# All matmuls of a fused convolution and feed-forward kernel in 64-row tiles

## Chip, cores, metric

The kernel runs on one core of one Trainium2 chip. The metric is device time in microseconds (us). The kernel before takes 831.15 us (median of 4 fast runs, 828.9 to 833.99). A ratio is the mean time of one kernel's fast runs over the mean time of the other's fast runs of the same rounds, so it is not quite the ratio of the medians quoted beside it.

Words used below. A *stage* is 512 tokens of each half of the batch, 1024 in all; there are 32, and a 33rd turn of the loop that only finishes the last output. A *unit* is a sixteenth of a stage on TensorE: one chunk of 128 hidden features of this stage, and half a block of 128 tokens of the previous stage's output. *Row tiling* is how many of the 128 rows of TensorE's array a matmul takes: all 128, or 64, and then two matmuls (a *pair*) can sit side by side. A *bank* is a part of PSUM, the memory that matmuls write to. The *span* runs from a core's first instruction to its last. PE is TensorE, PEld its weight loads, DVE VectorE, ACT ScalarE, POOL GpSimd, SP SyncE.

## The reference, cut

```python
# x: (8, 4096, 192), weight: (8 heads, 7 taps); 24 channels to a head
w = softmax(weight)                            # over the 7 taps of each head
conv[b,s,d] = sum_k w[head(d),k] * x[b, s-6+k, d]   # zeros ahead of the first token
h = conv @ w_in                                # 192 -> 2048
g = h * sigmoid(beta * h)
out = g @ w_out                                # 2048 -> 192
```

The contraction of the first product is 192 long: one and a half times the 128 rows of the array.

## The kernel before

The two halves of the batch (`h`) are computed together. The input tile of a stage has three column groups: group 0 and 1 are channels 0 to 127 of half 0 and of half 1 (128 partitions each), group 2 is channels 128 to 191 of both halves, half 0 on partitions 0 to 63 and half 1 on 64 to 127. So the hidden product is two matmuls of 128 rows and a pair of 64 rows that sit beside each other in the array.

```python
def hidden(s, fc):                 # one chunk of 128 hidden features
    ph = psum_h.tile([128, 2, TOK], FP32)             # bufs=3, one bank per half
    w = w_in_s[:, :, fc * 128 : (fc + 1) * 128]
    for h in range(2):
        nc.tensor.matmul(ph[:, h, :], w[:, 0, :], ct[:, h, :], start=True, stop=False)
    for h in range(2):
        rows = slice(h * DB, (h + 1) * DB)            # DB = 64
        nc.tensor.matmul(ph[:, h, :], w[rows, 1, :], ct[rows, 2, :], start=False, stop=True)
    nc.scalar.activation(g[:, fc, :, :], ph, AF.Silu, scale=beta[:, fc : fc + 1])

def output(s, part):               # half a block of 128 tokens: 8 of 16 chunks
    # ... (cut: which block, which half; po takes two blocks, one bank, bufs=2)
    for fc in range(half * NF // 2, (half + 1) * NF // 2):
        nc.tensor.matmul(po[:, q % 2, :], g[:, fc, h, q * BLK : (q + 1) * BLK],
                         w_out_s[:, fc, :], start=(fc == 0), stop=(fc == NF - 1))
    if part % 4 == 3:
        nc.vector.tensor_copy(osb[:, q - 1 : q + 1, :], po)
    # ... (cut: store after every fourth block)

for s in range(N_ST + 1):
    ops = conv_ops(s + 1)          # 14: seven taps on groups 0-1 (1024 wide), seven on group 2 (512)
    for u in range(NF):            # 16 units
        # ... (cut: weight preparation in stage 0)
        hidden(s, u)
        output(s - 1, u)
        if u < len(ops):
            ops[u]()               # VectorE: a tap of the next stage's convolution
        # ... (cut: cast of stage s+3 to bf16 in DRAM, transposing load of stage s+2)
```

The seven taps are one multiplication (TENSOR_SCALAR), five multiply-adds (SCALAR_TENSOR_TENSOR) and one addition (TENSOR_TENSOR) on VectorE.

Of the kernel before, what the change touches and what calls it, by code (L numbers as in the profile page):

```python
# [8 lines left out]
FP32 = mybir.dt.float32  # L9
BF16 = mybir.dt.bfloat16  # L10
AF = mybir.ActivationFunctionType
ALU = mybir.AluOpType
# [3 lines left out]
def kernel(  # L16
# [15 lines left out]
    nc = tc.nc  # L32

    B, S, D = x.shape
    H, K = weight.shape
    F = moe_w_in.shape[1]
    group = D // H
    DA = 128
    DB = D - DA
    TOK = 512  # L40
    NF = F // 128
    PAD = K - 1
    HALO = 16
    CHUNKS = S // TOK
    N_ST = (B // 2) * CHUNKS
    BLK = 128
    N_BLK = TOK // BLK


    x_v = x.rearrange("(h p) s d -> p s h d", h=2)  # L50
# [4 lines left out]
    consts = ctx.enter_context(tc.tile_pool(name="consts", bufs=1))  # L55
    setup = ctx.enter_context(tc.tile_pool(name="setup", bufs=1))
    xd_pool = ctx.enter_context(
        tc.tile_pool(name="xd", bufs=4, space=bass.MemoryType.DRAM)
    )
    xt_pool = ctx.enter_context(tc.tile_pool(name="xt", bufs=3))  # L60
    ct_pool = ctx.enter_context(tc.tile_pool(name="ct", bufs=2))
    g_pool = ctx.enter_context(tc.tile_pool(name="g", bufs=2))
    osb_pool = ctx.enter_context(tc.tile_pool(name="osb", bufs=3))
    psum_h = ctx.enter_context(
        tc.tile_pool(name="psum_h", bufs=3, space=bass.MemoryType.PSUM)
    )
    psum_o = ctx.enter_context(
        tc.tile_pool(name="psum_o", bufs=2, space=bass.MemoryType.PSUM)
    )
# [6 lines left out]
    def cast(s):  # L76
        p, c = divmod(s, CHUNKS)
        r0 = HALO if c == 0 else 0
        t0 = c * TOK - HALO + r0
        t1 = (c + 1) * TOK  # L80
        xd = xd_pool.tile([HALO + TOK, 3, DA], BF16, name="xd")
        nc.gpsimd.dma_start(out=xd[r0:, 0:2, :], in_=x_v[p, t0:t1, :, 0:DA])  # L82
        nc.gpsimd.dma_start(  # L83
            out=xd[r0:, 2, :].rearrange("t (h d) -> t h d", h=2),
            in_=x_v[p, t0:t1, :, DA:D],
        )
        xds[s] = xd

    def xpose(s):
        r0 = HALO if s % CHUNKS == 0 else 0  # L90
        xd = xds.pop(s)
        xt = xt_pool.tile([128, 3, HALO + TOK], BF16, name="xt")
        if r0:
            nc.vector.memset(xt[:, :, 0:HALO], 0.0)
        nc.sync.dma_start_transpose(  # L95
            xt[:, :, r0:], xd[r0:, :, :].rearrange("t c d -> t (c d)")
        )
        xts[s] = xt


    cw = consts.tile([128, 2, K], FP32)
    full = DA // group
    rest = DA - full * group

    def heads(rows, h0, h1, n):
        nc.scalar.dma_start(
            out=rows,
            in_=weight[h0:h1, :].unsqueeze(1).to_broadcast((h1 - h0, n, K)),
        )

    cast(0)
    heads(cw[0 : full * group, 0, :], 0, full, group)
    heads(cw[full * group : DA, 0, :], full, full + 1, rest)
    for h in range(2):
        o = h * DB
        heads(cw[o : o + group - rest, 1, :], full, full + 1, group - rest)
        heads(cw[o + group - rest : o + DB, 1, :], full + 1, H, group)
    beta_q = setup.tile([NF, 128], FP32)
    nc.scalar.dma_start(out=beta_q, in_=moe_beta.rearrange("(c p) -> c p", p=128))
    xpose(0)  # L120
# [5 lines left out]
    FW = F // NW  # L126
    w_in_raw = []
    for i in range(NW):
        raw = setup.tile([128, 2, FW], FP32, name=f"w_in_raw{i}")
        cols = slice(i * FW, (i + 1) * FW)  # L130
        nc.sync.dma_start(out=raw[:, 0, :], in_=moe_w_in[0:DA, cols])  # L131
        nc.sync.dma_start(out=raw[0:DB, 1, :], in_=moe_w_in[DA:D, cols])
        nc.sync.dma_start(out=raw[DB:128, 1, :], in_=moe_w_in[DA:D, cols])  # L133
        w_in_raw.append(raw)
    w_out_raw = setup.tile([128, NF, D], FP32)
    nc.sync.dma_start(  # L136
        out=w_out_raw, in_=moe_w_out.rearrange("(c p) d -> p c d", p=128)
# [2 lines left out]
    cast(2)  # L140
    xpose(1)

    nmax = setup.tile([128, 2], FP32)
    nc.vector.reduce_max(nmax, cw, axis=mybir.AxisListType.X, negate=True)  # L144
    for j in range(2):
        nc.scalar.activation(cw[:, j, :], cw[:, j, :], AF.Exp, bias=nmax[:, j : j + 1])  # L146
    ssum = setup.tile([128, 2], FP32)
    nc.vector.reduce_sum(ssum, cw, axis=mybir.AxisListType.X)
    rsum = setup.tile([128, 2], FP32)
    nc.vector.reciprocal(rsum, ssum)  # L150
    w_last = consts.tile([128, 2], FP32)
    nc.vector.tensor_tensor(w_last, cw[:, :, K - 1], rsum, ALU.mult)
    r_last = setup.tile([128, 2], FP32)
    nc.vector.reciprocal(r_last, cw[:, :, K - 1])
    for j in range(2):
        nc.vector.tensor_scalar_mul(cw[:, j, :], cw[:, j, :], r_last[:, j : j + 1])

    pb = psum_o.tile([128, NF], FP32, name="po")
    nc.tensor.transpose(pb, beta_q, ident)  # L159
    beta = consts.tile([128, NF], FP32)  # L160
    nc.vector.tensor_copy(beta, pb)  # L161
    beta_r = setup.tile([128, NF], FP32)
    nc.vector.reciprocal(beta_r, beta)

    w_in_s = consts.tile([128, 2, F], BF16)

    def prep_w_in(i):
        cols = slice(i * FW, (i + 1) * FW)
        for j in range(2):
            nc.vector.tensor_scalar_mul(  # L170
                w_in_s[:, j, cols], w_in_raw[i][:, j, :], w_last[:, j : j + 1]
            )

    w_out_s = consts.tile([128, NF, D], BF16)
# [8 lines left out]

    def conv_ops(s):
        xt = xts.pop(s)
        ct = ct_pool.tile([128, 3, TOK], BF16, name="ct")
        cts[s] = ct
        ops = []
        for j, cs in ((0, slice(0, 2)), (1, slice(2, 3))):

            def tap(k, j=j, cs=cs):
                src = xt[:, cs, HALO - PAD + k : HALO - PAD + k + TOK]
                dst = ct[:, cs, :]
                if k == 0:
                    nc.vector.tensor_scalar_mul(dst, src, cw[:, j, 0:1])  # L195
                elif k < K - 1:
                    nc.vector.scalar_tensor_tensor(  # L197
                        out=dst,
                        in0=src,
                        scalar=cw[:, j, k : k + 1],  # L200
                        in1=dst,
                        op0=ALU.mult,
                        op1=ALU.add,
                    )
                else:
                    nc.vector.tensor_tensor(dst, src, dst, ALU.add)  # L206

            ops += [lambda k=k, tap=tap: tap(k) for k in range(K)]
        return ops

    gs = {}

    def hidden(s, fc):
        ct, g = cts[s], gs[s]
        ph = psum_h.tile([128, 2, TOK], FP32, name="ph")
        w = w_in_s[:, :, fc * 128 : (fc + 1) * 128]
        for h in range(2):
            nc.tensor.matmul(ph[:, h, :], w[:, 0, :], ct[:, h, :], start=True, stop=False)  # L218
        for h in range(2):
            rows = slice(h * DB, (h + 1) * DB)  # L220
            nc.tensor.matmul(  # L221
                ph[:, h, :], w[rows, 1, :], ct[rows, 2, :], start=False, stop=True
            )
        nc.scalar.activation(g[:, fc, :, :], ph, AF.Silu, scale=beta[:, fc : fc + 1])  # L224

    pos, osbs = {}, {}

    def output(s, part):

        blk, half = divmod(part, 2)  # L230
        h, q = divmod(blk, N_BLK)
        g = gs[s]
        if part % 4 == 0:
            pos[s] = psum_o.tile([128, 2, D], FP32, name="po")
        if part % 8 == 0:
            osbs[s] = osb_pool.tile([128, N_BLK, D], FP32, name="osb")
        po, osb = pos[s], osbs[s]
        for fc in range(half * NF // 2, (half + 1) * NF // 2):
            nc.tensor.matmul(  # L239
                po[:, q % 2, :],  # L240
                g[:, fc, h, q * BLK : (q + 1) * BLK],
                w_out_s[:, fc, :],
                start=(fc == 0),
                stop=(fc == NF - 1),
            )
        if part % 4 == 3:
            nc.vector.tensor_copy(osb[:, q - 1 : q + 1, :], po)  # L247
        if part % 8 == 7:
            p, c = divmod(s, CHUNKS)
            nc.sync.dma_start(out=out_v[h, p, c], in_=osb)  # L250
# [4 lines left out]
    for s in range(N_ST + 1):  # L255
        if s < N_ST:
            gs[s] = g_pool.tile([128, NF, 2, TOK], BF16, name="g")
        ops = conv_ops(s + 1) if s + 1 < N_ST else []
        for u in range(NF):
            if s == 0 and u % (NF // NW) == 0:  # L260
                prep_w_in(u // (NF // NW))
            if s < N_ST:
                hidden(s, u)
            if s > 0:
                output(s - 1, u)
            if u < len(ops):
                ops[u]()
            if s == 0:
                prep_w_out(u)
            if u == 0 and s + 3 < N_ST:  # L270
                cast(s + 3)
            if u == 1 and s + 2 < N_ST:
                xpose(s + 2)
# [30 lines left out]
```

## Time and profile before

| what | before |
|---|---|
| median of 4 runs | 831.15 us |
| span of the profiled run | 829.9 us |
| first output matmul starts | 61.67 us |
| unit (period of the hidden matmuls) | 1.520 us, in all of the stream |
| last matmul starts | 825.21 us |

The unit is the time from one chunk's first hidden matmul to the next chunk's, taken from the start times in the trace; from the first output matmul on there are 495, and all lie within 0.01 us of 1.520.

These are lines of the page of the kernel before: busy time by engine (share of the span, instructions), the shares of the chain of waits by engine and line, and groups of instructions (busy us, mean ns of one, idle before).

```profile
PE 784.3 (95%) x6145; PEld 445.7 (54%) x6145; DVE 462.8 (56%) x613; ACT 572.7 (69%) x516; POOL 82.5 (10%) x70
...
PE 93%; DMA 4%; DVE 2%; SPq 1%; issue 0%; POOL 0%; POOLq 0%
PE po L239 47%; PE ph L218 26%; PE ph L221 20%; DMA xt<-xd 2%; DMA w_in_raw_107<-in_moe_w_in_dram 1%; DVE ct L197 1%; DMA xd<-in_x_dram 1%; DVE w_out_s L177 1%; DVE w_in_s L170 0%; SPq L95 0%; SPq L133 0%; SPq L131 0%; DVE ct L195 0%; DVE ct L206 0%; SPq L136 0%
...
L224 ACT ACTIVATE g<-ph,beta 128x1024 bf16<-128x1024 f32 x512 | 569.6, 1114 | 233.6 <-PE ph L221 233.6
L239 PE MATMUL po<-w_out_s,g 128*128 128x192 bf16 x4096 | 424.0, 247 | 0.0
...
L218 PE MATMUL ph<-ct,w_in_s 128*128 128x512 bf16 x1024 | 308.2, 383 | 31.1 <-DVE w_in_s L170 31.1
...
L247 DVE COPY osb<-po 128x384 f32<-128x384 f32 x128 | 71.4, 557 | 329.0 <-PE po L239 329.0
L221 PE MATMUL ph<-ct,w_in_s 64*128 64x512 bf16 x1024 | 201.7, 391 | 0.8 <-DVE w_in_s L170 0.8
```

PE is busy 95% of the span and 93% of the chain of waits; ACT has a 1.11 us activation to do in each unit. L218 are the 128-row hidden matmuls, L221 the 64-row ones, L239 the output. The mean ns of a matmul is its time from start to modelled end, with overlap, so it is not what a matmul costs in a stream. For that, starts are compared. This is the timeline of one unit (start us, us, engine, line, operation; `x2` merges two of a kind):

```profile
399.78 0.59 PE L218 MATMUL ph<-ct,w_in_s 128*128 128x512 bf16 x2
400.30 0.10 PEld L221 LDWEIGHTS <-w_in_s 64*128 64x128 bf16 x2 [0.42 <-issue]
400.30 0.39 PE L221 MATMUL ph<-ct,w_in_s 64*128 64x512 bf16 x2
400.62 0.61 PEld L239 LDWEIGHTS <-g 128*128 128x128 bf16 x8 [0.23 <-issue]
400.63 0.83 PE L239 MATMUL po<-w_out_s,g 128*128 128x192 bf16 x8
...
401.30 0.59 PE L218 MATMUL ph<-ct,w_in_s 128*128 128x512 bf16 x2
401.50 0.56 DVE L247 COPY osb<-po 128x384 f32<-128x384 f32 x1 [3.62 <-PE po L239]
```

From the first L218 at 399.78 to L221 at 400.30 pass 0.52 us for two matmuls of 512 columns. From L221 at 400.30 to L239 at 400.63 pass 0.33 us for a pair that runs as one. From L239 at 400.63 to the next L218 at 401.30 pass 0.67 us for eight matmuls of 192 columns. The single starts in the trace say what the stream costs: two 128-row matmuls start 216 ns apart (399.776 and 399.992), the two of the 64-row pair 3 ns apart (400.304 and 400.307), and the output matmuls 82.5 ns apart (the first two 93). Three times 216 and eight times 82.5 ns is 1.308 us. The unit takes 1.520. The missing 0.212 us lies at the two changes between 128-row and 64-row matmuls, ahead of the pair and behind it: PEld L221 and PEld L239 stand idle ahead of their loads (0.42 and 0.23 us, given to "issue", no semaphore), where the other loads run ahead of the matmul that they serve.

### The profile page before, as it was taken

The page shows a single profiled execution, that of the slowest core. Times are in us where ns is not written, and L with a number is a line of the kernel's source. Part 1 is how long each engine was busy: PE and PEld are TensorE (multiplying, and loading weights), DVE is VectorE, ACT ScalarE, POOL GpSimd, SP SyncE. Part 2 cuts the span into 40 slices and gives each one's busy share as a digit, 9 for nine tenths or more (in the row PEclk, how much of TensorE's full clock was granted, in tenths as well). Part 3 has the DMA queues.
Part 4 walks back from the last instruction along what each step waited for, and adds up shares of the span by engine and source line. Part 5 has one row for each costly group of instructions (what it writes and reads, how often), then busy time and mean ns, then how long its engine had stood idle before and what let it go on. Part 6 is the DMA issues. An engine that isn't in the chain of part 4 may idle for free.

```text
span 829.9 us, 13854 instructions
## 1 busy us (share of the span) xinstructions
PE 784.3 (95%) x6145; PEld 445.7 (54%) x6145; DVE 462.8 (56%) x613; ACT 572.7 (69%) x516; POOL 82.5 (10%) x70
## 2 busy tenths in 40 slices
PE   0279999999999999999999999999999999999997
PEld 0015555555555555555555555555555555555556
DVE  2696665555656556565555656555565665555601
ACT  1267777777777777777777777777777777777772
POOL 8389800000000000000000000000000000000000
PEclk9989999999999999999999999999999999999999
DMA  9999991210322221122222112222201322220111
GB/s 143 222 169 179 182 120 41 58 53 25 59 58 46 53 58 43 35 59 58 39 58 59 36 42 59 58 39 58 59 28 51 59 59 39 58 54 25 39 39 59
DMA packets 157341, 55.60 MB, mean 67 GB/s; under 512 B 121425, under 2 KB 156257, under 8 KB 157281
## 3 DMA queue, kind: packets, MB, share of 16 engines
q1 hardware_dynamic: 88592, 41.77, 22.1%
q0 software_dynamic: 68352, 12.93, 18.9%
q8 instruction: 48, 0.79, 0.4%
q10 hardware_dynamic: 337, 0.02, 0.0%
q14 instruction: 12, 0.10, 0.0%
HBM read 29.54 MB, written 38.09 MB: 81 GB/s over the span
## 4 chain that ended last, share of the span: by engine, by line
PE 93%; DMA 4%; DVE 2%; SPq 1%; issue 0%; POOL 0%; POOLq 0%
PE po L239 47%; PE ph L218 26%; PE ph L221 20%; DMA xt<-xd 2%; DMA w_in_raw_107<-in_moe_w_in_dram 1%; DVE ct L197 1%; DMA xd<-in_x_dram 1%; DVE w_out_s L177 1%; DVE w_in_s L170 0%; SPq L95 0%; SPq L133 0%; SPq L131 0%; DVE ct L195 0%; DVE ct L206 0%; SPq L136 0%
## 5 line engine op out<-in xcount | busy, mean ns | idle before, releaser
L224 ACT ACTIVATE g<-ph,beta 128x1024 bf16<-128x1024 f32 x512 | 569.6, 1114 | 233.6 <-PE ph L221 233.6
L239 PE MATMUL po<-w_out_s,g 128*128 128x192 bf16 x4096 | 424.0, 247 | 0.0
L239 PEld LDWEIGHTS <-g 128*128 128x128 bf16 x4096 | 312.4, 98 | 112.2 <-issue 112.2
L218 PE MATMUL ph<-ct,w_in_s 128*128 128x512 bf16 x1024 | 308.2, 383 | 31.1 <-DVE w_in_s L170 31.1
L197 DVE SCALAR_TENSOR_TENSOR ct<-xt,cw,ct 128x1024 bf16<-128x1024 bf16 (+1 forms) x320 | 325.1, 1016 | 8.8
L247 DVE COPY osb<-po 128x384 f32<-128x384 f32 x128 | 71.4, 557 | 329.0 <-PE po L239 329.0
L221 PE MATMUL ph<-ct,w_in_s 64*128 64x512 bf16 x1024 | 201.7, 391 | 0.8 <-DVE w_in_s L170 0.8
L221 PEld LDWEIGHTS <-w_in_s 64*128 64x128 bf16 x1024 | 49.3, 93 | 221.3 <-issue 217.8
L218 PEld LDWEIGHTS <-w_in_s 128*128 128x128 bf16 x1024 | 91.3, 98 | 36.8 <-DVE w_in_s L170 32.3
L82 POOL DMA_DIRECT2D xd<-in_x_dram x32 | 42.6, 1330 | 12.4 <-DMA xd<-in_x_dram 11.6
L83 POOL DMA_DIRECT2D xd<-in_x_dram x32 | 42.5, 1327 | 8.3 <-DMA xd<-in_x_dram 7.9
L206 DVE TENSOR_TENSOR ct<-xt,ct 128x1024 bf16<-128x1024 bf16 x64 | 35.7, 557 | 2.1
L195 DVE TENSOR_SCALAR ct<-xt,cw 128x1024 bf16<-128x1024 bf16 x64 | 27.6, 431 | 14.1 <-DMA xt<-xd 13.3
L177 DVE TENSOR_SCALAR w_out_s<-w_out_raw,beta_r 128x192 bf16<-128x192 f32 x16 | 8.9, 568 | 0.0
L159 PE MATMUL po<-ident,beta_q 16*128 16x16 f32 x1 | 0.3, 254 | 9.2 <-DMA beta_q<-in_moe_beta_dram 9.2
L146 ACT ACT_TABLE_LOAD x1 | 1.3, 1283 | 6.1 <-DMA cw<-in_weight_dram 6.1
L159 PEld LDWEIGHTS po<-ident,beta_q 16*128 16x128 f32 x1 | 0.2, 176 | 9.1 <-issue 9.1
L144 DVE TENSOR_REDUCE nmax<-cw 128x2 f32<-128x14 f32 x1 | 0.2, 168 | 7.7 <-DMA cw<-in_weight_dram 7.7
L224 ACT ACT_TABLE_LOAD x1 | 1.3, 1283 | 1.5 <-DVE beta L161 1.5
L170 DVE TENSOR_SCALAR w_in_s<-w_in_raw_115,w_last 128x512 bf16<-128x512 f32 x2 | 1.5, 800 | 0.0
L146 ACT ACTIVATE cw<-cw,nmax 128x7 f32<-128x7 f32 x2 | 0.5, 294 | 1.4 <-DVE nmax L144 1.4
L170 DVE TENSOR_SCALAR w_in_s<-w_in_raw_111,w_last 128x512 bf16<-128x512 f32 x2 | 1.5, 774 | 0.0
(16 smaller groups left out, 4.7 us busy)
## 6 DMA issues: line engine op xcount, KB each, us to landing
out_dram<-osb SPq DMA_DIRECT2D x64, 384.0 KB, 3.0
xd<-in_x_dram POOLq DMA_DIRECT2D x28, 264.0 KB, 10.1
xd<-in_x_dram POOLq DMA_DIRECT2D x28, 132.0 KB, 10.2
w_out_raw<-in_moe_w_out_dram SPq DMA_DIRECT2D x1, 1536.0 KB, 12.8
xd<-in_x_dram POOLq DMA_DIRECT2D x4, 256.0 KB, 9.1
xd<-in_x_dram POOLq DMA_DIRECT2D x4, 128.0 KB, 8.7
xt<-xd SPq DMA_TRANSPOSE x32, 4.6
w_in_raw_103<-in_moe_w_in_dram SPq DMA_DIRECT2D x1, 256.0 KB
```

The costliest lines, as they stand in the source:

```text
L82: nc.gpsimd.dma_start(out=xd[r0:, 0:2, :], in_=x_v[p, t0:t1, :, 0:DA])
L83: nc.gpsimd.dma_start(out=xd[r0:, 2, :].rearrange("t (h d) -> t h d", h=2), in_=x_v[p, t0:t1, :, DA:D],)
L170: nc.vector.tensor_scalar_mul(w_in_s[:, j, cols], w_in_raw[i][:, j, :], w_last[:, j : j + 1])
L177: nc.vector.tensor_scalar_mul(w_out_s[:, c, :], w_out_raw[:, c, :], beta_r[:, c : c + 1])
L195: nc.vector.tensor_scalar_mul(dst, src, cw[:, j, 0:1])
L197: nc.vector.scalar_tensor_tensor(out=dst, in0=src, scalar=cw[:, j, k : k + 1], in1=dst, op0=ALU.mult, op1=ALU.add,)
L206: nc.vector.tensor_tensor(dst, src, dst, ALU.add)
L218: nc.tensor.matmul(ph[:, h, :], w[:, 0, :], ct[:, h, :], start=True, stop=False)
L221: nc.tensor.matmul(ph[:, h, :], w[rows, 1, :], ct[rows, 2, :], start=False, stop=True)
L224: nc.scalar.activation(g[:, fc, :, :], ph, AF.Silu, scale=beta[:, fc : fc + 1])
L239: nc.tensor.matmul(po[:, q % 2, :], g[:, fc, h, q * BLK : (q + 1) * BLK], w_out_s[:, fc, :], start=(fc == 0), stop=(fc == NF - 1),)
L247: nc.vector.tensor_copy(osb[:, q - 1 : q + 1, :], po)
```

## The change

The intent: no change of the array's row tiling is left in the loop. Each partition half holds one batch half in all three groups of 64 channels, so the hidden product is three 64-row pairs. The contraction of the output product (128 hidden features) is split as well: rows 0 to 63 into one PSUM bank, rows 64 to 127 into another, and VectorE adds the two. So the two tiles of a pair never write to one bank. `po` grows to two banks, so `ph` goes from three buffers to two. Every group of 64 channels now has its own heads on the same partitions, so the taps are 21 of width 512 instead of 14, and they are spread over all 16 units.

```diff
 def hidden(s, fc):
-    w = w_in_s[:, :, fc * 128 : (fc + 1) * 128]
-    for h in range(2):
-        nc.tensor.matmul(ph[:, h, :], w[:, 0, :], ct[:, h, :], start=True, stop=False)
-    for h in range(2):
-        rows = slice(h * DB, (h + 1) * DB)
-        nc.tensor.matmul(
-            ph[:, h, :], w[rows, 1, :], ct[rows, 2, :], start=False, stop=True
-        )
+    cols = slice(fc * 128, (fc + 1) * 128)
+    for j in range(NG):                       # NG = 3 groups of DG = 64 channels
+        for h in range(2):
+            rows = slice(h * DG, (h + 1) * DG)
+            nc.tensor.matmul(ph[:, h, :], w_in_s[rows, j, cols], ct[rows, j, :],
+                             start=(j == 0), stop=(j == NG - 1))
...
 def output(s, part):
+    b = quarter // 2
+    for fc in range((quarter % 2) * NF // 2, (quarter % 2 + 1) * NF // 2):
+        for r in range(2):
+            rows = slice(r * 64, (r + 1) * 64)
+            nc.tensor.matmul(po[:, r, b * D : (b + 1) * D],
+                             g[rows, fc, h, (q + b) * BLK : (q + b + 1) * BLK],
+                             w_out_s[rows, fc, :],
+                             start=(fc == 0), stop=(fc == NF - 1))
+    if quarter == 3:
+        dst = osb[:, q : q + 2, :].rearrange("p b d -> p (b d)")
+        nc.vector.tensor_copy(dst, po[:, 0, 0 : 2 * D])
+        nc.vector.tensor_tensor(dst, po[:, 1, 0 : 2 * D], dst, ALU.add)
...
             hidden(s, u)
             output(s - 1, u)
-            if u < len(ops):
-                ops[u]()
+            for op in ops[u * len(ops) // NF : (u + 1) * len(ops) // NF]:
+                op()
... (cut: psum_h bufs 3 -> 2; po two banks; the casts write the new layout in pieces of
...  64 channels; w_in is loaded to both partition halves, 3 MB instead of 2 MB; the
...  conv weights are loaded in 14 small loads instead of 6; scaling per group)
```

More of the change, by code (lines that the diff above doesn't have):

```diff
@@ L37 @@
     group = D // H
-    DA = 128
-    DB = D - DA
+    DG = 64
+    NG = D // DG
     TOK = 512
@@ L64 @@
     psum_h = ctx.enter_context(
-        tc.tile_pool(name="psum_h", bufs=3, space=bass.MemoryType.PSUM)
+        tc.tile_pool(name="psum_h", bufs=2, space=bass.MemoryType.PSUM)
     )
@@ L80, in cast @@
         t1 = (c + 1) * TOK
-        xd = xd_pool.tile([HALO + TOK, 3, DA], BF16, name="xd")
-        nc.gpsimd.dma_start(out=xd[r0:, 0:2, :], in_=x_v[p, t0:t1, :, 0:DA])
-        nc.gpsimd.dma_start(
-            out=xd[r0:, 2, :].rearrange("t (h d) -> t h d", h=2),
-            in_=x_v[p, t0:t1, :, DA:D],
-        )
+        xd = xd_pool.tile([HALO + TOK, NG, 2, DG], BF16, name="xd")
+        for h in range(2):
+            nc.gpsimd.dma_start(
+                out=xd[r0:, :, h, :],
+                in_=x_v[p, t0:t1, h, :].rearrange("t (c d) -> t c d", c=NG),
+            )
         xds[s] = xd
@@ L91, in xpose @@
         xd = xds.pop(s)
-        xt = xt_pool.tile([128, 3, HALO + TOK], BF16, name="xt")
+        xt = xt_pool.tile([128, NG, HALO + TOK], BF16, name="xt")
         if r0:
@@ L95, in xpose @@
         nc.sync.dma_start_transpose(
-            xt[:, :, r0:], xd[r0:, :, :].rearrange("t c d -> t (c d)")
+            xt[:, :, r0:], xd[r0:].rearrange("t c h d -> t (c h d)")
         )
         xts[s] = xt
-    cw = consts.tile([128, 2, K], FP32)
-    full = DA // group
-    rest = DA - full * group
-    def heads(rows, h0, h1, n):
-        nc.scalar.dma_start(
-            out=rows,
-            in_=weight[h0:h1, :].unsqueeze(1).to_broadcast((h1 - h0, n, K)),
-        )
+    cw = consts.tile([128, NG, K], FP32)
     cast(0)
-    heads(cw[0 : full * group, 0, :], 0, full, group)
-    heads(cw[full * group : DA, 0, :], full, full + 1, rest)
     for h in range(2):
-        o = h * DB
-        heads(cw[o : o + group - rest, 1, :], full, full + 1, group - rest)
-        heads(cw[o + group - rest : o + DB, 1, :], full + 1, H, group)
+        for c in range(NG):
+            d = c * DG
+            while d < (c + 1) * DG:
+                head = d // group
+                end = min((head + 1) * group, (c + 1) * DG)
+                n = 1
+                if d % group == 0 and end - d == group:
+                    n = ((c + 1) * DG - d) // group
+                    end = d + n * group
+                o = h * DG - c * DG
+                nc.scalar.dma_start(
+                    out=cw[o + d : o + end, c, :],
+                    in_=weight[head : head + n, :]
+                    .unsqueeze(1)
+                    .to_broadcast((n, (end - d) // n, K)),
+                )
+                d = end
     beta_q = setup.tile([NF, 128], FP32)
@@ L128 @@
     for i in range(NW):
-        raw = setup.tile([128, 2, FW], FP32, name=f"w_in_raw{i}")
+        raw = setup.tile([128, NG, FW], FP32, name=f"w_in_raw{i}")
         cols = slice(i * FW, (i + 1) * FW)
-        nc.sync.dma_start(out=raw[:, 0, :], in_=moe_w_in[0:DA, cols])
-        nc.sync.dma_start(out=raw[0:DB, 1, :], in_=moe_w_in[DA:D, cols])
-        nc.sync.dma_start(out=raw[DB:128, 1, :], in_=moe_w_in[DA:D, cols])
+        for h in range(2):
+            nc.sync.dma_start(
+                out=raw[h * DG : (h + 1) * DG, :, :],
+                in_=moe_w_in[:, cols].rearrange("(c d) f -> d c f", c=NG),
+            )
         w_in_raw.append(raw)
@@ L141 @@
     xpose(1)
-    nmax = setup.tile([128, 2], FP32)
+    nmax = setup.tile([128, NG], FP32)
     nc.vector.reduce_max(nmax, cw, axis=mybir.AxisListType.X, negate=True)
-    for j in range(2):
+    for j in range(NG):
         nc.scalar.activation(cw[:, j, :], cw[:, j, :], AF.Exp, bias=nmax[:, j : j + 1])
-    ssum = setup.tile([128, 2], FP32)
+    ssum = setup.tile([128, NG], FP32)
     nc.vector.reduce_sum(ssum, cw, axis=mybir.AxisListType.X)
-    rsum = setup.tile([128, 2], FP32)
+    rsum = setup.tile([128, NG], FP32)
     nc.vector.reciprocal(rsum, ssum)
-    w_last = consts.tile([128, 2], FP32)
+    w_last = consts.tile([128, NG], FP32)
     nc.vector.tensor_tensor(w_last, cw[:, :, K - 1], rsum, ALU.mult)
-    r_last = setup.tile([128, 2], FP32)
+    r_last = setup.tile([128, NG], FP32)
     nc.vector.reciprocal(r_last, cw[:, :, K - 1])
-    for j in range(2):
+    for j in range(NG):
         nc.vector.tensor_scalar_mul(cw[:, j, :], cw[:, j, :], r_last[:, j : j + 1])
-    pb = psum_o.tile([128, NF], FP32, name="po")
+    pb = psum_o.tile([128, 2, TOK], FP32, name="po")[:, 0, 0:NF]
     nc.tensor.transpose(pb, beta_q, ident)
@@ L163 @@
     nc.vector.reciprocal(beta_r, beta)
-    w_in_s = consts.tile([128, 2, F], BF16)
+    w_in_s = consts.tile([128, NG, F], BF16)
     def prep_w_in(i):
         cols = slice(i * FW, (i + 1) * FW)
-        for j in range(2):
+        for j in range(NG):
             nc.vector.tensor_scalar_mul(
@@ L185, in conv_ops, with tap @@
         xt = xts.pop(s)
-        ct = ct_pool.tile([128, 3, TOK], BF16, name="ct")
+        ct = ct_pool.tile([128, NG, TOK], BF16, name="ct")
         cts[s] = ct
         ops = []
-        for j, cs in ((0, slice(0, 2)), (1, slice(2, 3))):
-            def tap(k, j=j, cs=cs):
-                src = xt[:, cs, HALO - PAD + k : HALO - PAD + k + TOK]
-                dst = ct[:, cs, :]
+        for j in range(NG):
+            def tap(k, j=j):
+                src = xt[:, j, HALO - PAD + k : HALO - PAD + k + TOK]
+                dst = ct[:, j, :]
                 if k == 0:
@@ L215, in hidden @@
         ph = psum_h.tile([128, 2, TOK], FP32, name="ph")
-        w = w_in_s[:, :, fc * 128 : (fc + 1) * 128]
-        for h in range(2):
-            nc.tensor.matmul(ph[:, h, :], w[:, 0, :], ct[:, h, :], start=True, stop=False)
-        for h in range(2):
-            rows = slice(h * DB, (h + 1) * DB)
-            nc.tensor.matmul(
-                ph[:, h, :], w[rows, 1, :], ct[rows, 2, :], start=False, stop=True
-            )
+        cols = slice(fc * 128, (fc + 1) * 128)
+        for j in range(NG):
+            for h in range(2):
+                rows = slice(h * DG, (h + 1) * DG)
+                nc.tensor.matmul(
+                    ph[:, h, :],
+                    w_in_s[rows, j, cols],
+                    ct[rows, j, :],
+                    start=(j == 0),
+                    stop=(j == NG - 1),
+                )
         nc.scalar.activation(g[:, fc, :, :], ph, AF.Silu, scale=beta[:, fc : fc + 1])
@@ L228, in output @@
     def output(s, part):
-        blk, half = divmod(part, 2)
-        h, q = divmod(blk, N_BLK)
+        pair, quarter = divmod(part, 4)
+        h, q = divmod(2 * pair, N_BLK)
         g = gs[s]
-        if part % 4 == 0:
-            pos[s] = psum_o.tile([128, 2, D], FP32, name="po")
+        if quarter == 0:
+            pos[s] = psum_o.tile([128, 2, TOK], FP32, name="po")
         if part % 8 == 0:
@@ L237, in output @@
         po, osb = pos[s], osbs[s]
-        for fc in range(half * NF // 2, (half + 1) * NF // 2):
-            nc.tensor.matmul(
-                po[:, q % 2, :],
-                g[:, fc, h, q * BLK : (q + 1) * BLK],
-                w_out_s[:, fc, :],
-                start=(fc == 0),
-                stop=(fc == NF - 1),
-            )
-        if part % 4 == 3:
-            nc.vector.tensor_copy(osb[:, q - 1 : q + 1, :], po)
+        b = quarter // 2
+        for fc in range((quarter % 2) * NF // 2, (quarter % 2 + 1) * NF // 2):
+            for r in range(2):
+                rows = slice(r * 64, (r + 1) * 64)
+                nc.tensor.matmul(
+                    po[:, r, b * D : (b + 1) * D],
+                    g[rows, fc, h, (q + b) * BLK : (q + b + 1) * BLK],
+                    w_out_s[rows, fc, :],
+                    start=(fc == 0),
+                    stop=(fc == NF - 1),
+                )
+        if quarter == 3:
+            dst = osb[:, q : q + 2, :].rearrange("p b d -> p (b d)")
+            nc.vector.tensor_copy(dst, po[:, 0, 0 : 2 * D])
+            nc.vector.tensor_tensor(dst, po[:, 1, 0 : 2 * D], dst, ALU.add)
         if part % 8 == 7:
```

## The prediction

> **What bounds it now.** TensorE: PE is 95% busy, ACT 69%, DVE 56%; the chain of waits is 93% PE. In the timeline at 400 us one unit (one hidden chunk plus half a block's output) repeats every 1.52 us: two 128-row x512 matmuls 216 ns apart, a pair of 64-row x512 that start 3 ns apart and run together, eight 128-row x192 82.5 ns apart. Streaming is 3x216 + 8x82.5 = 1.31 us. The other 0.21 us is two gaps: last 128-row hidden matmul to pair 307 ns where 216 is the stream; pair to first output matmul 322 ns. The Trainium skill, "TensorEngine Tiling (Array Packing)", Key Properties, says a change of tiling mode drains the array; gaps of about 0.1 us agree.
>
> **What the change does.**
> 1. PE: no mode switches left. Hidden becomes three 64-row pairs (648 ns), output eight pairs x192 (660 ns): the same streaming if each pair runs as today's does. Instructions per unit rise from 24 to 44. The skill, "TensorE: Matmul & The Clock Gate", Part 3, has weight loads overlap matmuls of other row groups; this trace's pair agrees (loads 4 ns apart, 93 ns each), but shows no long stream of pairs. I expect a unit of 1.31 to 1.37 us, 1.33 central. Over 31 stages x 16 units 94 us saved, all on the critical path.
> 2. DVE: a tap on 1024 (1283 ns) and one on 512 (749 ns) become three on 512: 1.4 us more a stage. Four evacuations a stage each gain an add, about the copy's 557 ns. 14.4 becomes 18 us of a 23 us stage: no throughput limit.
> 3. Order on DVE: 14 taps were issued in units 0 to 13; now 21 spread to unit 15, so the last two (749 and 424 ns) stand behind the last output block's copy and add, which wait for PE's last matmul of the stage. The next stage's first hidden chunk needs those taps. Today the copy starts 0.29 us after that last matmul's start; then copy, add, two taps: 2.0 to 2.3 us. PE can meanwhile do only groups 0 and 1 of the next chunk (0.43 us). New stall: about 2.0 us at 31 stage ends, 62 us. It was zero.
> 4. Start: w_in is loaded 1.5 times (+1 MB at roughly 200 GB/s, 5 us), its scaling takes three operations instead of two, taps cost more, casts move 1.5 times the packets. I expect +7 us.
> 5. ph has two buffers, not three: the activation (1114 ns) ends well before its buffer is due again after 2.66 us. No cost.
>
> **Sum.** 832.7 - 94 + 62 + 7 = 808 us. Range 785 to 850. Faster by over 2%: 0.57; within 2%: 0.26; slower: 0.17.
>
> **What would show it.** Unit period in the timeline near 1.33 us; a PE idle of about 2 us once per stage at the hidden matmul, released by DVE's last tap on ct, some 60 us in the table of waits; copy and add together about 1.1 us; no PE wait on ACT; first output matmul near 68 us instead of 61.7.
>
> **What would make it wrong.** If pairs do not sustain (a weight-load or dispatch limit: 44 instructions a unit), a unit of 1.41 us cancels the gain and 1.5 makes a loss. If the taps landed before the last copy, no stall: about 750 us. If the PE clock falls after each stall, the loss is larger.

## The result

| what | before | after |
|---|---|---|
| median us (4 runs each) | 831.15 | 796.99 |
| ratio, 95% interval | | 0.959, 0.9554 to 0.9626 |
| span of the profiled run | 829.9 | 796.4 |
| first output matmul starts | 61.67 | 69.73 |
| unit | 1.520 | 1.308 |
| stage end: what the first unit of a stage takes beyond a unit | none | 2.10 us, 30 times |
| last matmul starts | 825.21 | 791.16 |
| instructions of the core | 13854 | 24460 |

The result is correct and in the range. These are the lines of the page of the kernel after that answer to those of before (L226 is now all of the hidden product, L251 the output, L260 and L261 copy and add):

```profile
PE 682.7 (86%) x11265; PEld 512.3 (64%) x11265; DVE 573.1 (72%) x970; ACT 573.1 (72%) x517; POOL 59.0 (7%) x70
...
PE 82%; DVE 11%; DMA 5%; POOL 1%; issue 1%; ACT 0%; POOLq 0%
PE po L251 42%; PE ph L226 40%; DVE ct L202 3%; DMA xt<-xd 3%; DVE osb L260 2%; DVE osb L261 2%; DMA xd<-in_x_dram 2%; DVE ct L211 2%; POOL xd L83 1%; DVE w_in_s L175 1%; DVE w_out_s L182 0%; ACT g L233 0%; DVE ct L200 0%; POOL ident masks.py:199 0%; POOL ident masks.py:197 0%
...
L233 ACT ACTIVATE g<-ph,beta 128x1024 bf16<-128x1024 f32 x512 | 569.9, 1114 | 183.0 <-PE ph L226 179.0
L226 PE MATMUL ph<-ct,w_in_s 64*128 64x512 bf16 x3072 | 433.6, 380 | 83.6 <-DVE ct L211 57.8
...
L251 PE MATMUL po<-w_out_s,g 64*128 64x192 bf16 x8192 | 427.0, 243 | 0.0
...
L260 DVE COPY osb<-po 128x384 f32<-128x384 f32 x128 | 71.5, 558 | 167.4 <-PE po L251 167.3
L261 DVE TENSOR_TENSOR osb<-po,osb 128x384 f32<-128x384 f32 x128 | 71.4, 557 | 4.4
```

PE fell to 86% busy and 82% of the chain; DVE is now 11% of the chain, where it was 2% and all of that in the start. One unit in the timeline of the kernel after:

```profile
400.54 0.83 PE L226 MATMUL ph<-ct,w_in_s 64*128 64x512 bf16 x6
...
400.98 0.82 PEld L251 LDWEIGHTS <-g 64*128 64x128 bf16 x16
...
401.19 0.84 PE L251 MATMUL po<-w_out_s,g 64*128 64x192 bf16 x16
...
401.85 0.83 PE L226 MATMUL ph<-ct,w_in_s 64*128 64x512 bf16 x6
```

Three hidden pairs from 400.54 to 401.19 and eight output pairs from 401.19 to 401.85: 1.31 us, and no idle time noted ahead of any group. The stream of pairs holds: in the trace, two output matmuls of one pair start 19 to 20 ns apart, and pairs follow each other after 82.5 ns, exactly as the single 128-row matmuls did. Now the end of a stage, in the same columns:

```profile
411.65 0.84 PE L251 MATMUL po<-w_out_s,g 64*128 64x192 bf16 x16
...
412.31 0.61 PE L226 MATMUL ph<-ct,w_in_s 64*128 64x512 bf16 x4
412.53 0.56 DVE L260 COPY osb<-po 128x384 f32<-128x384 f32 x1 [0.67 <-PE po L251]
413.12 0.56 DVE L261 TENSOR_TENSOR osb<-po,osb 128x384 f32<-128x384 f32 x1
413.60 0.74 DVE L202 SCALAR_TENSOR_TENSOR ct<-xt,cw,ct 128x512 bf16<-128x512 bf16 x1
...
414.37 0.42 DVE L211 TENSOR_TENSOR ct<-xt,ct 128x512 bf16<-128x512 bf16 x1
...
414.85 0.39 PE L226 MATMUL ph<-ct,w_in_s 64*128 64x512 bf16 x2 [1.93 <-DVE ct L211]
...
415.06 0.84 PE L251 MATMUL po<-w_out_s,g 64*128 64x192 bf16 x16
```

The output block of L251 begins at 411.65 and is the stage's last. The next stage's first chunk starts at 412.31 and does four of its six matmuls. The last two wait till 414.85, "1.93 <-DVE ct L211". DVE shows why: copy (L260), add (L261), a multiply-add tap (L202) and the last tap (L211), one behind the other, from 412.53 to 414.79. PE's table of waits (us in total, times, longest):

```profile
PE ph L226 <- DVE ct L211: 57.8, 30, 1.9
...
PE ph L226 <- ACT g L233: 1.4, 4, 0.5
```

Past the start, all of PE's waiting is this one wait, 30 times. (It gives 57.8 us, counted from the modelled end of the matmul before; counted by starts, a first unit takes 3.41 us instead of 1.308, so 30 x 2.10 = 63 us are lost.) The four waits on ACT all lie before 70 us, in the start.

The parts add up in the two profiled runs. The unit gives 496 x 0.212 = 105.2 us back. The stage ends take 63.0. The start takes 69.73 - 61.67 = 8.1. The end takes 0.6 more, from the last matmul's start to the end of the span (5.3 us against 4.7), about the size of the add. 829.9 - 105.2 + 63.0 + 8.1 + 0.6 = 796.4, which is the span.

### The profile page after: what moved, and what is told of

The parts are those of the page before. It is cut to its first block, busy times and chain, and to the rows that moved or that the text cites. A ratio compares the mean times of both kernels' runs of the same rounds, so it can differ in the third digit from the quotient of the medians.

```text
span 796.4 us, 24460 instructions
## 1 busy us (share of the span) xinstructions
PE 682.7 (86%) x11265; PEld 512.3 (64%) x11265; DVE 573.1 (72%) x970; ACT 573.1 (72%) x517; POOL 59.0 (7%) x70
## 4 chain that ended last, share of the span: by engine, by line
PE 82%; DVE 11%; DMA 5%; POOL 1%; issue 1%; ACT 0%; POOLq 0%
PE po L251 42%; PE ph L226 40%; DVE ct L202 3%; DMA xt<-xd 3%; DVE osb L260 2%; DVE osb L261 2%; DMA xd<-in_x_dram 2%; DVE ct L211 2%; POOL xd L83 1%; DVE w_in_s L175 1%; DVE w_out_s L182 0%; ACT g L233 0%; DVE ct L200 0%; POOL ident masks.py:199 0%; POOL ident masks.py:197 0%
## 5 line engine op out<-in xcount | busy, mean ns | idle before, releaser
L226 PE MATMUL ph<-ct,w_in_s 64*128 64x512 bf16 x3072 | 433.6, 380 | 83.6 <-DVE ct L211 57.8
L251 PEld LDWEIGHTS <-g 64*128 64x128 bf16 x8192 | 368.6, 94 | 98.2
L251 PE MATMUL po<-w_out_s,g 64*128 64x192 bf16 x8192 | 427.0, 243 | 0.0
L202 DVE SCALAR_TENSOR_TENSOR ct<-xt,cw,ct 128x512 bf16<-128x512 bf16 x480 | 359.8, 749 | 13.3
L226 PEld LDWEIGHTS <-w_in_s 64*128 64x128 bf16 x3072 | 161.7, 95 | 155.6 <-issue 75.5
L260 DVE COPY osb<-po 128x384 f32<-128x384 f32 x128 | 71.5, 558 | 167.4 <-PE po L251 167.3
L261 DVE TENSOR_TENSOR osb<-po,osb 128x384 f32<-128x384 f32 x128 | 71.4, 557 | 4.4
L83 POOL DMA_DIRECT2D xd<-in_x_dram x64 | 58.6, 922 | 58.2 <-DMA xd<-in_x_dram 53.8
L211 DVE TENSOR_TENSOR ct<-xt,ct 128x512 bf16<-128x512 bf16 x96 | 40.7, 424 | 3.2
L200 DVE TENSOR_SCALAR ct<-xt,cw 128x512 bf16<-128x512 bf16 x96 | 33.7, 351 | 5.3 <-DMA xt<-xd 5.3
L151 ACT ACT_TABLE_LOAD x1 | 1.3, 1283 | 19.9 <-DMA cw<-in_weight_dram 19.9
L175 DVE TENSOR_SCALAR w_in_s<-w_in_raw_117,w_last 128x512 bf16<-128x512 f32 x3 | 2.0, 728 | 0.0
L175 DVE TENSOR_SCALAR w_in_s<-w_in_raw_120,w_last 128x512 bf16<-128x512 f32 x3 | 1.6, 596 | 0.0
L175 DVE TENSOR_SCALAR w_in_s<-w_in_raw_114,w_last 128x512 bf16<-128x512 f32 x3 | 1.3, 483 | 0.0
L175 DVE TENSOR_SCALAR w_in_s<-w_in_raw_111,w_last 128x512 bf16<-128x512 f32 x3 | 1.3, 480 | 0.0
```

The costliest lines, as they stand in the source:

```text
L83: nc.gpsimd.dma_start(out=xd[r0:, :, h, :], in_=x_v[p, t0:t1, h, :].rearrange("t (c d) -> t c d", c=NG),)
L151: nc.scalar.activation(cw[:, j, :], cw[:, j, :], AF.Exp, bias=nmax[:, j : j + 1])
L175: nc.vector.tensor_scalar_mul(w_in_s[:, j, cols], w_in_raw[i][:, j, :], w_last[:, j : j + 1])
L200: nc.vector.tensor_scalar_mul(dst, src, cw[:, j, 0:1])
L202: nc.vector.scalar_tensor_tensor(out=dst, in0=src, scalar=cw[:, j, k : k + 1], in1=dst, op0=ALU.mult, op1=ALU.add,)
L211: nc.vector.tensor_tensor(dst, src, dst, ALU.add)
```

## The experiments

The theory after the traces: (1) the gain of a unit is what the two changes of the row tiling cost (the texts call it a drain: the array runs empty), and nothing else about 64-row matmuls; (2) the stage end is an order on VectorE, not VectorE's load; (3) the start is later by what is loaded there. Each had a rival. Eleven kernels ran. The medians of before in the three groups of rounds are 830.64, 832.69 and 829.27 us; all ratios are against before of the same rounds. Each group ran on another chip, so medians of two groups can differ by about 2 us without a cause in the kernel; there the ratios are the better measure.

| kernel | median us | ratio (95%) |
|---|---|---|
| e1_taps_first | 735.54 | 0.886 (0.8843 to 0.8876) |
| e2_no_add (wrong) | 777.88 | 0.9369 (0.9351 to 0.9387) |
| e3_full_out | 881.86 | 1.0618 (1.0596 to 1.0641) |
| e4_before_in_twos | 778.72 | 0.9372 (0.934 to 0.9404) |
| e5_before_out64 | 834.95 | 1.0034 (0.9998 to 1.0071) |
| s1_cw_two_queues | 731.59 | 0.8797 (0.8771 to 0.8822) |
| s2_xpose_early | 734.78 | 0.8833 (0.8807 to 0.886) |
| s3_both | 729.74 | 0.8781 (0.8753 to 0.8809) |
| f1_casts_paced | 723.39 | 0.8718 (0.8699 to 0.8738) |
| f2_before_more_w_in | 833.28 | 1.0042 (1.0019 to 1.0064) |
| f3_before_more_cw | 834.90 | 1.0064 (1.0045 to 1.0083) |

### The unit: what a change of row tiling costs

**e3_full_out.** From the kernel after; the output goes back to 128-row matmuls.

```diff
-            for r in range(2):
-                rows = slice(r * 64, (r + 1) * 64)
-                nc.tensor.matmul(po[:, r, b * D : (b + 1) * D], g[rows, fc, h, ...],
-                                 w_out_s[rows, fc, :], ...)
+            nc.tensor.matmul(po[:, 0, b * D : (b + 1) * D], g[:, fc, h, ...],
+                             w_out_s[:, fc, :], ...)
-            nc.vector.tensor_tensor(dst, po[:, 1, 0 : 2 * D], dst, ALU.add)
```

> The kernel after with the output product in 128-row matmuls, one bank and no add; the hidden product stays in 64-row pairs. It has two changes of the row tiling in each unit, as the kernel before. Theory (drain at each change): unit 648 + 660 + 2 x 106 = about 1.52 us, stage end 1.54 us more, time about 884 us, worse than the kernel before. Rival (64-row pairs are the faster in themselves, by their weight loads): the hidden half keeps its share of the gain, the unit is near 1.41 us and the time near 830 us or less.

Measured: unit 1.520 us, 881.86 us. A timeline of its PE (L226 hidden in pairs, L249 output in 128 rows):

```profile
400.29 0.82 PE L226 MATMUL ph<-ct,w_in_s 64*128 64x512 bf16 x6
...
401.04 0.83 PE L249 MATMUL po<-w_out_s,g 128*128 128x192 bf16 x8
...
401.81 0.60 PE L226 MATMUL ph<-ct,w_in_s 64*128 64x512 bf16 x4
```

Hidden to output now takes 0.75 us where the three pairs take 0.65, output to hidden 0.77 where eight matmuls take 0.66: about 0.1 us at each change, in both directions. Half of the change brings none of the gain. It even leaves the kernel 6% slower than before, since the stage ends (30 times 1.405 us, 1.54 expected) and the later start (7.9 us) stay. A stage end costs less than in e2 below, which has the same chain on VectorE; the gap of the change that would have come there anyway may run inside the wait, but nothing was run to show that.

**e4_before_in_twos.** From the kernel before; two chunks go together, so a pair of changes serves two units.

```diff
-    def hidden(s, fc):
+    def hidden(s, fcs):                       # two chunks
+        for fc in fcs:                        # their four 128-row matmuls
+            ph = phs[fc] = psum_h.tile([128, 2, TOK], FP32, name="ph")
+            ...
+        for fc in fcs:                        # then their two 64-row pairs
+            ...
-            hidden(s, u); output(s - 1, u)
+            if u % 2 == 0:
+                hidden(s, (u, u + 1)); output(s - 1, u); output(s - 1, u + 1)
```

> The kernel before with two hidden chunks issued together: first their four 128-row matmuls, then their two 64-row pairs, then sixteen output matmuls. The same matmuls and tiles, but one pair of changes of the row tiling in two units instead of one. Theory (about 0.106 us at each change, whatever stands between): two units take 2 x 1.308 + 0.212 = 2.83 us instead of 3.04, the time falls by 496 x 0.106 = 52 us to about 780. Rival (the gaps belong to each 64-row pair or to accumulation onto the same bank, not to the change): no fall, about 831 us.

Measured: 2.827 us for two units in the whole stream, 778.72 us. The matmuls, tiles and shapes are those of before; only how often the tiling changes differs. Its PE (L226 the 64-row pairs, L220 the 128-row matmuls, L244 the output):

```profile
400.07 0.61 PE L226 MATMUL ph<-ct,w_in_s 64*128 64x512 bf16 x4
...
400.61 1.49 PE L244 MATMUL po<-w_out_s,g 128*128 128x192 bf16 x16
...
401.94 1.03 PE L220 MATMUL ph<-ct,w_in_s 128*128 128x512 bf16 x4
...
402.90 0.60 PE L226 MATMUL ph<-ct,w_in_s 64*128 64x512 bf16 x4
```

From 400.07 to 402.90 is one period. This is the sharpest test of the theory: half of the changes, half of the loss. The rival of accumulation falls in the kernel after as well, where three pairs accumulate onto the same two banks 216 ns apart without a gap. And this reordering alone, with no new tiling, is 18 us faster than the kernel after, which still pays its stage ends.

**e5_before_out64.** From the kernel before; only the output is put into 64-row pairs with two banks and the add, `ph` has two buffers, and everything else stays, the order of the taps too. So the hidden product still changes the tiling twice a unit.

```diff
-                psum_h ... bufs=3
+                psum_h ... bufs=2
-    def output(s, part): ...        # as before
+    def output(s, part): ...        # as in the kernel after
```

> The kernel before with the output product alone in 64-row pairs, two banks and the add, and with two ph buffers; its hidden product, its tap order (taps in units 0 to 13) and its start are kept. Theory (drain at each change of row tiling): still two changes a unit, after the two 128-row matmuls and ahead of them, so the unit stays 1.52 us; add and third ph buffer are off the chain, no stage-end stall: 831 us, within 1%. Rival (64-row output pairs are faster or slower in themselves, or add and lost buffer cost time): a unit other than 1.52 us or stage ends that stand out.

Measured: unit 1.520 us, no stage end stands out, ratio 1.0034 with 1 inside the interval. (Some records of hidden matmuls are missing in this trace; but from the first output matmul to the last pass 763.54 us, as in before, to 0.01 us.) So each half of the change alone leaves the unit at 1.520 us; only both together take it to 1.308. The add and the lost buffer cost nothing in the stream. Theory (1) holds in all three runs, as a cost of about 0.106 us at each change. Why a change costs that is not shown: within one tiling a weight load starts 2 ns behind the start of the matmul before it (399.778 and 399.776 in before), at a change 307 ns behind it (400.299 and 399.992). An array that has to run empty, or a load that can't be issued ahead, would both look like this, and no run tells them apart.

### The stage end: order or load

**e1_taps_first.** From the kernel after; the same instructions, with a unit's taps issued ahead of its output block.

```diff
             hidden(s, u)
+            for op in ops[u * len(ops) // NF : (u + 1) * len(ops) // NF]:
+                op()
             output(s - 1, u)
-            for op in ops[u * len(ops) // NF : (u + 1) * len(ops) // NF]:
-                op()
```

> The kernel after, with each unit's taps issued on VectorE ahead of that unit's output block instead of behind it; the same instructions, only their order on VectorE differs. Theory (order): the 2.10 us that 30 stage ends cost is the chain copy, add, two taps behind the stage's last matmul; with the taps ahead of the copy all 63 us go, no stage end differs from the unit of 1.308 us, and the time is about 797 - 63 = 734 us. Rival (throughput): VectorE, at 18 us of work a stage, is too full; then the waits on the taps come back at other places and the time stays above 770 us.

Measured: 735.54 us, 61 us below the kernel after, and every stage end down from 2.10 us to 0.025. The same place in a stage as above (in e1's trace):

```profile
381.85 0.84 PE L251 MATMUL po<-w_out_s,g 64*128 64x192 bf16 x16
...
382.49 0.42 DVE L211 TENSOR_TENSOR ct<-xt,ct 128x512 bf16<-128x512 bf16 x1
382.51 0.85 PE L226 MATMUL ph<-ct,w_in_s 64*128 64x512 bf16 x6
382.84 0.55 DVE L260 COPY osb<-po 128x384 f32<-128x384 f32 x1
...
383.19 0.84 PE L251 MATMUL po<-w_out_s,g 64*128 64x192 bf16 x16
```

L211 now ends at 382.91, ahead of the copy L260, and the six hidden matmuls of L226 at 382.51 run on. It ends just in time: the third pair is due 0.43 us after 382.51, which is the likely source of the 25 ns. VectorE has 571 us of work in this run as it had 573 in the kernel after, at 78% of the span instead of 72%. The load was not the limit.

**e2_no_add.** From the kernel after without the add; the output is wrong.

```diff
-            nc.vector.tensor_tensor(dst, po[:, 1, 0 : 2 * D], dst, ALU.add)
```

> The kernel after without the add on VectorE, so the second bank is never read and the result is wrong on purpose. Theory (order): the chain at a stage end loses the add's 0.56 us and nothing else: each of 30 stage ends costs 1.54 us instead of 2.10, the unit stays 1.308 us, the time falls by about 17 us to 780. Rival (throughput): 2.2 us of VectorE work a stage fall away, so up to 66 us come back.

Measured: a stage end costs 1.51 us instead of 2.10 and the unit stays 1.308; 777.88 us, 19 us less than the kernel after. The add was 0.59 us of each stage end, which is the step from the copy's start to the add's in the timeline above (412.53 to 413.12), and nothing more. Both runs bear theory (2) out; the rival falls.

### The start

The first output matmul comes 8.1 us later than before. The prediction had given 5 of 7 us to 1 MB more of w_in. The traces show something else besides. Before (the queue of the small loads on ACT; the first use of the conv weights, `nmax`; and the first tap of the second input tile, each with the wait ahead of it):

```profile
0.74 4.77 ACTq L106 DMA_DIRECT2D cw<-in_weight_dram  x6
...
8.62 0.17 DVE L144 TENSOR_REDUCE nmax<-cw 128x2 f32<-128x14 f32 x1 [7.73 <-DMA cw<-in_weight_dram]
...
37.74 0.49 DVE L195 TENSOR_SCALAR ct<-xt,cw 128x1024 bf16<-128x1024 bf16 x1 [7.64 <-DMA xt<-xd]
```

After:

```profile
0.74 18.62 ACTq L114 DMA_DIRECT2D cw<-in_weight_dram  x14
...
24.93 0.18 DVE L149 TENSOR_REDUCE nmax<-cw 128x3 f32<-128x21 f32 x1 [24.04 <-DMA cw<-in_weight_dram]
...
47.84 0.35 DVE L200 TENSOR_SCALAR ct<-xt,cw 128x512 bf16<-128x512 bf16 x1 [5.35 <-DMA xt<-xd]
```

ACT was through with its 14 conv-weight loads 18.62 us after it began, and `nmax` came at 24.93 instead of 8.62 us. Only 9.5 of the 18.62 us are issuing (4.6 us for the six before), for the line merges loads across gaps. In the trace the loads of ACT and SyncE share eight semaphores in turn, and a load waits until the one before it on its semaphore has landed. The 13th small load waited 8.2 us for the first transposed tile (landed at 18.07, load issued at 18.09). The second tile was waited for till 47.84 instead of 37.74.

**f2_before_more_w_in.** From the kernel before; 1 MB more is loaded and never read.

```diff
         nc.sync.dma_start(out=raw[DB:128, 1, :], in_=moe_w_in[DA:D, cols])
+        more = setup.tile([128, FW], FP32, name=f"more{i}")
+        nc.sync.dma_start(out=more, in_=moe_w_in[0:128, cols])
```

> The kernel before with 1 MB more loaded in the start, a third 256 KB load behind the two groups of each quarter of w_in, never read: the bytes that the change adds there. Theory of the prediction (1 MB at about 200 GB/s, all ahead of the second tile's transpose): first output matmul about 5 us later, 66.7 us, and 836 us. Rival (the number of small conv-weight loads makes the start later): within 1.5 us of before.

Measured: first output matmul at 63.60 us (+1.9), ratio 1.0042, which is 3.5 us of 829 (1.6 to 5.3 by the interval). The bytes cost something, by the middle value less than the 5 us expected, which the interval does not rule out. Against the rival (within 1.5 us) speaks the time; the +1.9 of one profile is too near to it.

**f3_before_more_cw.** From the kernel before; the six conv-weight loads are split by head into twelve, with the same bytes.

```diff
-        nc.scalar.dma_start(out=rows,
-            in_=weight[h0:h1, :].unsqueeze(1).to_broadcast((h1 - h0, n, K)))
+        for i, o in enumerate(range(h0, h1)):
+            nc.scalar.dma_start(out=rows[i * n : (i + 1) * n, :],
+                in_=weight[o : o + 1, :].unsqueeze(1).to_broadcast((1, n, K)))
```

> The kernel before with its six conv-weight loads split by head into twelve, the same bytes to the same places (the kernel after has fourteen). Theory of the prediction (bytes make the start later; the count of small loads was left out of it): first output matmul within 1.5 us of 61.7 us. Rival (small loads make it later): conv weights land at 15 us or later instead of 7 to 8, w_in's issue on SyncE is held up, first output matmul 3 to 5 us later, about 835 us.

Measured: first output matmul at 65.29 us (+3.6), ratio 1.0064, which is 5.3 us (3.7 to 6.9). The same three lines of its start (the wait of `nmax` is put down to beta_q, which shares a semaphore with a conv-weight load):

```profile
0.74 16.50 ACTq L107 DMA_DIRECT2D cw<-in_weight_dram  x12
...
21.96 0.17 DVE L145 TENSOR_REDUCE nmax<-cw 128x2 f32<-128x14 f32 x1 [21.06 <-DMA beta_q<-in_moe_beta_dram]
...
41.46 0.49 DVE L196 TENSOR_SCALAR ct<-xt,cw 128x1024 bf16<-128x1024 bf16 x1 [4.27 <-DMA xt<-xd]
```

So a count of small loads that the prediction left out is a term of about the size of the bytes that it named. It works as in the kernel after: the 12th small load waited 7.2 us for the first transposed tile, on its semaphore. The two terms are not added up: a single profile places the start only to about 3 us (e5, whose loads are those of before, had its first output matmul at 64.41 us, before at 61.67, e4 at 61.41).

A third term was not tested alone. From the issue of the second tile's transpose to its first tap pass 16.4 to 17.7 us in the five traces with the old casts (before, e4, e5, f2, f3; f2 has the bytes of the new w_in), and 19.9 to 21.7 in after, e1, e2, e3 and s1, where each cast moves 1.5 times the packets. So some 4 us of the second tile's 10 us delay go with the casts; the prediction named their packets, without a number of their own.

**s1_cw_two_queues, s2_xpose_early, s3_both.** From e1; the start mended in parts.

```diff
 s1: half of the conv-weight loads from SyncE
-                nc.scalar.dma_start(out=cw[...], ...)
+                (nc.scalar if h == 0 else nc.sync).dma_start(out=cw[...], ...)
 s2: the second tile's cast and transpose earlier
     cast(0)
+    cast(1)
     ...
         w_in_raw.append(raw)
+        if i == 0:
+            xpose(1)
     ...
-    cast(1)
     cast(2)
-    xpose(1)
 s3: both
```

> The taps-first kernel with the conv weights of the second half issued from SyncE instead of all 14 small loads from ScalarE; they landed at 24.8 us, against 7.7 us in the kernel before. Theory (the start is set by the second transposed input tile, which lands at 47 us whatever the conv weights do): weights land near 14 us, the first hidden matmul comes 8 to 11 us earlier, but the first output matmul stays within 1 us of 69 us and the time within 2 us of 735. Rival (the 14 loads set the start): 6 us or more are gained.

> The taps-first kernel with the second input tile's cast issued right behind the first and its transpose right behind the first quarter of w_in, instead of behind all of w_in and w_out. Theory (second tile sets the start): it lands before VectorE is through with the first tile's taps at 42 us, so VectorE no longer waits about 5 us there and stage 1 starts 4 to 5 us earlier: about 731 us. Rival (the weights' bytes set the start): w_in comes later by as much, no gain.

> Both of these start changes on the taps-first kernel. Theory (conv weights and second tile each wait behind other transfers, and VectorE then needs about 14 us for the first tile and 21 us for stage 0): with both moved, VectorE starts near 17 us and is through near 54 to 58 us instead of 69: about 722 to 725 us. Rival (transfers as a whole bound the start): less than the sum of the two single runs' gains plus 2 us.

Measured: s1 735.54 to 731.59 us, first output matmul from 69.02 to 64.58 us. The expectation for s1 was wrong, and its reason with it: with the small loads spread, the issue of the second tile's transpose came at 20.83 instead of 27.37 us too, and the tile's first tap at 42.53 instead of 47.32. (The 24.8 and 7.7 us in its text are the lengths of the waits of `nmax` in e1 and before, not times of landing.) In the kernel after, SyncE issued no load between 12.2 and 20.2 us, and took up again just after ACT's last small load (19.36 us). The two are only near in time: the load that SyncE then issued had waited for a semaphore on which w_in's own first load landed at 20.15 us; in f3 the same gap ends at 17.82, that landing at 17.81. At other places SyncE did wait for small loads to land, 3.2 us in all in the kernel after and 4.2 in e1. s2 gained little: under 1 us by the medians, 0.3 us at the first output matmul (69.02 to 68.76), and by ratio not clear of e1, whose interval overlaps. VectorE no longer waited for the tile but for w_out (w_out_s, 4.9 us), which now landed last. s3 reached 729.74, not 722 to 725: again VectorE waited 9.5 us for w_out, till 41.66. The rival of s3 (the transfers as a whole bound the start) fits better.

**f1_casts_paced.** From s3; the casts from the fourth on wait for the taps of the stage that issues them, through a two-element copy.

```diff
             if u == 0 and s + 3 < N_ST:
+                nc.gpsimd.tensor_copy(gate, cts[s][0:1, NG - 1, 0:2])
                 cast(s + 3)
```

> The kernel with the taps first and both start changes, and each cast from the fourth on held back by a two-element copy on GpSimd that reads the taps of the stage that issues it (until now nothing held the casts back, and all 32 ran in the first 120 us). Theory (the start is bound by the transfers as a whole, and the early casts crowd out w_out, which landed at 41.6 us): w_out lands near 32 to 36 us, the first output matmul comes at 55 to 59 us instead of 63.5, about 723 us. Rival (w_in and w_out set their own landing): first output matmul within 1 us of 63.5, 729 to 730 us.

Measured: 723.39 us, first output matmul at 57.15 us, w_out first used at 37.70 instead of 41.66, a little later than the 32 to 36 expected. Casts of stages far ahead had been crowding out w_out; of the 6.3 us at the first output matmul that is 4, and the rest was not traced. This is the best version found: ratio 0.8718 against before.

## Why the prediction was right

- **The unit.** Predicted 1.33 us central, 1.31 to 1.37; measured 1.308. The 94 us saved were 105. The mechanism, a cost at each of two changes, held in e3, e4 and e5; whether it is a drain stays open. The margin put on top of the stream for 44 instructions a unit was not needed. The prediction's remark that a unit of 1.41 us would cancel the gain does not follow from its own terms: 69 us of costs over 496 units cancel it at 1.38. Nor did the clock fall: the granted clock was 1.00 from 100 to 700 us in both.
- **The stage end.** Predicted about 2.0 us 31 times, 62 us, by copy, add and two taps behind the last matmul; measured 2.10 us 30 times, 63 us (the first stage end falls in the start). e1 removed it by order alone, e2 shortened it by the add alone.
- **VectorE no throughput limit.** Predicted 18 us a stage; in the stretch from 100 to 700 us DVE was busy 457 of 600 us, so 17.6 of a stage's 23.0. e1 shows that it fits a stage of 20.95 as well, barely: the last tap comes just in time.
- **The start.** Predicted +7, measured +8.1 in the profiled run. The size was about right by luck, for the terms were not: 5 us for the bytes measured 1.9 us at the first output matmul and 3.5 us in the time (f2), and the doubled count of small loads, which the prediction did not have, measured 3.6 and 5.3 us (f3). The longer wait for the second tile behind the new casts has no run of its own.
- **Two ph buffers.** Predicted no cost; PE waited for ACT 1.4 us in all, in the start; e5 shows 0.3, in the start too.
- **The sum.** Predicted 808, measured 797. The unit, sized at 1.33 instead of 1.308, is 496 x 0.022 = 11 us of it. The rest cancels: stage ends, start and end came out about 3 us longer, and the value of 832.7 that the sum starts from, the median of three runs of before, was 1.6 above the later 831.15.

## What to carry to other kernels

Where matmuls of different row tiling alternate in a tight loop, count the changes: group equal tilings, or put everything into one tiling, and do it all the way, for half of it brought nothing here. When work is spread more evenly over an in-order engine, look at what then stands behind the last wait of each round: issuing each unit's taps ahead of its copy and add was worth nearly twice the whole change's gain (61 against 34 us). In a start, count the small loads as well as the bytes, and look at what each load waits for before it is issued.

## What the Trainium skill lacked or had wrong

- "TensorEngine Tiling (Array Packing)", Key Properties, says that a change of tiling mode drains the array, with no number. Here a change between 128-row and 64-row tiles cost about 0.1 us, 0.212 us a pair of changes (unit 1.520 against 1.308 us; e4, with a pair for two units, 2.827 us for two).
- "TensorE: Matmul & The Clock Gate", Back-to-back issue gap, gives a sustained 131 ns per matmul at 512 columns for a stream of weight load and matmul, and says that columns over 2.4 plus 2.5 ns over-counts there. Here 128-row matmuls of 512 columns, each with its load, started 216 ns apart and those of 192 columns 82.5 ns apart, which is that formula at both sizes. The runs decide for the formula.
- The same page, Part 3, gives speed-ups of single groups of packed matmuls and 4 ns from start to start. It has nothing on a long stream of two 64-row tiles. Here the starts in a pair were 19 to 20 ns apart in the kernel after (3 to 4 ns in before, e3 and e5), yet pairs followed each other every 82.5 or 216 ns with a load for every matmul: nothing was lost against 128-row matmuls.
- "DMA: Bandwidth & Descriptors", Issuing engines are not separate DMA queues, says that issuing from several engines only saves the time of initiating, usually small relative to the DMA itself. That is not all that it saved here: sharing 14 small loads with SyncE brought `nmax` from 25.70 to 13.30 us and 4 us of the time (s1 against e1), but issuing them had taken ACT only 9.5 us; 8.3 us more was a wait for the first transposed tile, on a shared semaphore, which s1 no longer had ahead of the small loads.
